# One dS unit in eight turned by TensorE instead of the crossbar, in the attention backward of an adaLN transformer block

## The chip, the cores and the metric

The kernel runs on one core of a Trainium2 chip. The metric is the device time of one execution in microseconds. The kernel before took 2854.23 us, the median of four runs (2842.84, 2850.54, 2857.91, 2863.89). The core has five engines that run side by side: TensorE (PE, matrix products, with its weight loads listed apart as PEld), VectorE (DVE), ScalarE (ACT), GpSimd (POOL) and SyncE (SP, which here issues most DMAs). SBUF is the working memory; PSUM holds the results of matmuls in eight banks of 2 KB per partition.

## The reference

A transformer block with adaptive layer norm (one sequence of 2048 tokens, width 512, 32 heads of 16) is run forward and backward; the outputs are the block's result and the gradients of nine inputs.

```python
scale = Dh ** (-0.5)                       # Dh = 16, H = 32
scores = einsum('bhqd,bhkd->bhqk', q, k) * scale
p = softmax(scores)
o = einsum('bhqk,bhkd->bhqd', p, v)
...
x = x + ga * (o @ wo)                      # o with the heads side by side
h = layernorm(x) * (1 + cb) + sb
x = x + gb * (relu(h @ w1 + b1) ** 2 @ w2 + b2)
_out, _vjp = jax.vjp(_f, A_x, A_wqkv, A_wo, B_w1, B_b1, B_w2, B_b2, c, w_mod)
return (_out, *_vjp(grad_out))
```

The part that matters here is the backward of the attention: with P the probabilities, it needs dV = P^T dO, dP = dO V^T, dS = P * (dP - rowsum(dO * O)), dQ = dS K and dK = dS^T Q, for each head a 2048 x 2048 matrix of scores.

## The kernel before

The forward, the MLP and its backward take the first 1256 us or so, the attention backward (`attn_bwd`) the next 1444, and `phase6`, the input and weight gradients, the rest.

`attn_bwd` loops over eight quads of heads (`g`), two pairs of heads in each (`jp`), four chunks of 512 keys (`c`) and 16 blocks of 128 queries (`ib`). One turn of the innermost loop is called a unit here: 8 x 2 x 4 x 16 = 1024 units, each with two heads (`a`). Four units with the same chunk (`G = 4`) form a group: 256 groups. Queries lie on the partitions, keys in the free dimension.

For a unit the program issues, in this order:
- for each of the two heads, the scores (L1265, a matmul of 64 rows into a `st` bank of PSUM) and the dP of the unit before (L1218, into half of a `dp` tile; the softmax correction is folded into extra rows of the operands). The `st` pool has two banks, so the exponentials free them one by one; `dp` has two tiles.
- on ScalarE the exponential of each head's scores (L1269, 128x512, PSUM to SBUF, into `pu`)
- on VectorE the product dS = dP * P of the unit before (L1223, 128x1024, into a quarter of the `ds` tile of its group). `ds` has three buffers.
- after every second unit, the dK and dV matmuls of two earlier units (`kv`, L1179, eight matmuls); after the units between, the dQ matmuls of two earlier units (`dq`, L1199, 16 matmuls).

dK and dV use dS as it lies. dQ needs it turned, with keys on the partitions. After the product of a group's fourth unit, which stands in the first unit of the next group, SP issues one DMA transpose of the whole group, through the crossbar on the way from SBUF to SBUF (L1227: 128 x 4096 elements into the 32 blocks of 128x128 of a `dsT` tile, four buffers). The dQ matmuls wait in a list (`pendq`) until more than eight units stand in it, and so a group's dQ is issued in the first and third unit of the third group after it. SP's queue holds, besides the 256 transposes, the loads of the next heads' operands, one between two groups.

After the last query block of a chunk VectorE scales and copies the dK/dV sums (L1182, `kvT`, 64 times); after the last chunk of a pair of heads `turn` transposes the whole of `kvT` on TensorE (L1188, 16 transposes into a `dp` tile) and ScalarE copies the result out twice (L1192), 16 times in all.

TensorE and SP keep the order written in the program. VectorE and ScalarE follow the order in which the program's tiles become ready to the framework, and each waits on semaphores of the engines it depends on.

Of the kernel before, what the change touches and what calls it, by code (L numbers as in the profile page):

```python
# [18 lines left out]
P = 128  # L19
# [68 lines left out]
class K:  # L88
# [1060 lines left out]
    def attn_bwd(self):  # L1149
# [9 lines left out]
        G = 4  # L1159
        W = 4 * DH  # L1160
        with ExitStack() as es:
            dtp = es.enter_context(tc.tile_pool(name="p5dt", bufs=4))
            kvp = es.enter_context(tc.tile_pool(name="p5kv", bufs=1))
            stp = es.enter_context(tc.tile_pool(name="p5st", bufs=2, space=PSUM))
            dpp = es.enter_context(tc.tile_pool(name="p5dp", bufs=2, space=PSUM))
            accp = es.enter_context(tc.tile_pool(name="p5acc", bufs=1, space=PSUM))
            acckv = accp.tile([P, 512], F32, name="acckv")
            nc.vector.memset(acckv[:], 0.0)
            accq = accp.tile([P, ST, 2, DH], F32, name="accq")
            masked, kvs = self.masked, self.kvs  # L1170
            pend, pendq = [], []

            def kv(u):
                (T, g, jp, c, ib, kvT, pu, ds) = u
                for j, (n, src) in enumerate((("Q", ds), ("dO", pu))):
                    for a in range(2):
                        r = 64 * j + 32 * a
                        col = (2 * jp + a) * DH
                        nc.tensor.matmul(acckv[r:r + DH, :], lhsT=T[n][:, ib, col:col + DH], rhs=src[:, a, :],  # L1179
                                         start=(ib == 0), stop=(ib == ST - 1))  # L1180
                if ib == ST - 1:
                    nc.vector.tensor_scalar(kvT[:, 512 * c:512 * (c + 1)], acckv[:], kvs[:], None, ALU.mult)  # L1182

            def turn(g, jp, kvT):
                h0 = 4 * g + 2 * jp
                tp = dpp.tile([P, ST, P], BF16, name="dp")
                for st in range(ST):
                    nc.tensor.transpose(tp[:, st, :], kvT[:, st * P:(st + 1) * P], self.ident[:])  # L1188
                v = tp[:].rearrange("p s (t a e) -> p t s a e", t=2, a=2)
                for t, dst in enumerate((self.dk_t, self.dv_t)):  # L1190
                    d = dst[:, :, h0 * DH:(h0 + 2) * DH].rearrange("p s (a d) -> p s a d", a=2)
                    nc.scalar.copy(d, v[:, t, :, :, 0:DH])  # L1192

            def dq(u, heads):
                (T, g, jp, c, ib, i, dsT) = u
                for a in heads:
                    col = (2 * jp + a) * DH
                    for sub in range(4):
                        nc.tensor.matmul(accq[:, ib, a, :], lhsT=dsT[:, (i * 2 + a) * 4 + sub, :],  # L1199
                                         rhs=T["K"][:, 4 * c + sub, col:col + DH],  # L1200
                                         start=(c == 0 and ib == 0 and a == 0 and sub == 0), stop=False,
                                         skip_group_check=True)
                if c == SC - 1 and ib == ST - 1 and 1 in heads:
                    h0 = 4 * g + 2 * jp
                    d = self.dq_t[:, :, h0 * DH:(h0 + 2) * DH].rearrange("p s (a d) -> p s a d", a=2)
                    nc.vector.tensor_scalar(d, accq[:], self.scale, None, ALU.mult)

            def kv_two():
                for u in pend[:2]:
                    kv(u)  # L1210
                (T, g, jp, c, ib, kvT, pu, ds) = pend[1]
                del pend[:2]
                return (g, jp, kvT) if c == SC - 1 and ib == ST - 1 else None

            def dP(dp, u, a):
                (T, g, jp, c, ib, kvT, pu, dsg, i) = u
                rd = slice(64 - 64 * jp, 128 - 64 * jp)
                nc.tensor.matmul(dp[:, a, :], lhsT=T["dOT"][rd, ib * P:(ib + 1) * P],  # L1218
                                 rhs=masked["VT"][2 * jp + a][rd, 512 * c:512 * (c + 1)], start=True, stop=True)

            def dS(dp, u):
                (T, g, jp, c, ib, kvT, pu, dsg, i) = u
                nc.vector.tensor_tensor(dsg[:, i], dp[:], pu[:], ALU.mult)  # L1223
                pend.append((T, g, jp, c, ib, kvT, pu, dsg[:, i]))
                if i == G - 1:
                    dsT = dtp.tile([P, 8 * G, P], BF16, name="dsT")
                    nc.sync.dma_start_transpose(dsT[:], dsg[:].rearrange("p i a k -> p (i a k)"))  # L1227
                    for i in range(G):
                        pendq.append((T, g, jp, c, ib - G + 1 + i, i, dsT))

            T = self.T0
            turnq, last = [], None
            for g in range(NQ):
                for jp in range(2):
                    pieces = []
                    if jp == 0:
                        pieces = self.pair_pieces(g, 1)
                    elif g + 1 == NQ:
                        for st in range(0, ST, 2):
                            pieces.append((self.xhat1_6[:, st:st + 2, :], self.xhat1_d.rearrange("(st p) d -> p st d", p=P)[:, st:st + 2, :]))  # L1240
                        for kt in range(self.DT):
                            pieces.append((self.wq_6[:, kt, :], self.io["A_wqkv"][kt * P:(kt + 1) * P, :]))
                    else:
                        Tn, pieces = self.load_group(g + 1)
                        pieces = self.pair_pieces(g + 1, 0) + pieces
                    kvT = kvp.tile([P, S], BF16, name="kvT")
                    for c in range(SC):
                        c0 = 512 * c
                        for ib0 in range(0, ST, G):
                            if pieces and (c or ib0):  # L1250
                                nc.sync.dma_start(*pieces.pop(0))
                            dsg = self.dsp.tile([P, G, 2, 512], BF16, name="ds")
                            for i in range(G):
                                ib = ib0 + i
                                q = slice(ib * P, (ib + 1) * P)
                                if turnq and i == 2:
                                    turn(*turnq.pop(0))
                                pu = self.pup.tile([P, 2, 512], BF16, name="pu")

                                if last:  # L1260
                                    dp = dpp.tile([P, 2, 512], F32, name="dp")
                                for a in range(2):
                                    stt = stp.tile([P, 512], F32, name="st")
                                    rs = slice(64 * jp, 64 * jp + 64)
                                    nc.tensor.matmul(stt[:], lhsT=T["QT"][rs, q], rhs=masked["KT"][2 * jp + a][rs, c0:c0 + 512],  # L1265
                                                     start=True, stop=True)
                                    if last:
                                        dP(dp, last, a)
                                    nc.scalar.activation(pu[:, a, :], stt[:], ACT.Exp, scale=self.scale)  # L1269
                                if last:  # L1270
                                    dS(dp, last)
                                last = (T, g, jp, c, ib, kvT, pu, dsg, i)
                                if i % 2 == 1 and len(pend) >= 4:
                                    r = kv_two()
                                    if r:
                                        turnq.append(r)
                                elif i % 2 == 0 and len(pendq) > 2 * G:
                                    for _ in range(4 if len(pendq) > 3 * G else 2):
                                        dq(pendq.pop(0), [0, 1])
                T = Tn  # L1280
            dp = dpp.tile([P, 2, 512], F32, name="dp")
            for a in range(2):
                dP(dp, last, a)
            dS(dp, last)
            while len(pend) > 2:
                kv_two()
            turn(*kv_two())
            while pendq:
                dq(pendq.pop(0), [0, 1])
# [254 lines left out]
```

The softmax here doesn't subtract the row's maximum and nothing guards it: scores larger than these inputs give would overflow.

## Time and profile before

| | |
|---|---|
| median of four runs | 2854.23 us |
| profiled execution | 2841.99 us (span 2840.2) |
| TensorE busy | 2518.3 us, 89% |
| ScalarE busy | 2214.8 us, 78% |
| VectorE busy | 1787.5 us, 63% |
| exponentials of the backward, L1269 | 1109.0 us, 2048 of 595 ns |
| dS products, L1223 | 1213.9 us, 1024 of 1220 ns |
| dsT transposes by DMA, L1227 | 256, median 8.0 us from issue to landing |
| mean granted TensorE clock | 0.966 |

Busy times of one engine add up only where its instructions do not overlap: an exponential of 595 ns starts some 0.54 us after the one before. "Idle before" is the time that an engine stood still just ahead of an instruction, and the name after the arrow is what ended it. A matmul's shown length (0.39 us for 512 columns) is longer than the distance between two of them, and two that use different halves of the array lie beside each other. SP's transposes show some 5.3 us each, which holds their wait for the products.

### The profile page before, as it was taken

Reading aid. Unit: us, or ns where it says so; the run is one execution under the profiler, and the core shown is the slowest. Engines: PE = TensorE matmul, PEld = TensorE weight load, DVE = VectorE, ACT = ScalarE, POOL = GpSimd, SP = SyncE. Lnnn points to the kernel's source line nnn. Section 1 sums busy time; section 2 is a strip of 40 time slices with the busy share of each in tenths; the row PEclk is TensorE's granted clock in tenths of the full one; section 3 lists DMA queues with packets and bytes.
Section 4 is the critical chain, followed back from the end, with each engine's and each line's share of the span. In section 5 each row is a group of like instructions: output and inputs, shape, how many; then the busy total and the mean of one; then the engine's idle time right before and its main releaser. Section 6 shows DMA issues by size and latency. Waiting matters only on the chain. (4 is left out here: it accounts for less than half of the span.)

```text
span 2840.2 us, 72244 instructions
## 1 busy us (share of the span) xinstructions
PE 2518.3 (89%) x29963; PEld 1212.8 (43%) x30186; DVE 1787.5 (63%) x2712; ACT 2214.8 (78%) x3376; POOL 361.3 (13%) x633
## 2 busy tenths in 40 slices
PE   5999799999999989979888888888888889899897
PEld 2555455555555545723333333333333333333343
DVE  4222323323312345649898888998988989889847
ACT  4999799999999975238787777887877878778623
POOL 2244201310321122420000000000000000000021
PEclk9999899999999999989999999999999999999999
DMA  4367743420631355989999999999999999999977
GB/s 150 89 148 161 156 89 90 119 67 20 152 86 40 101 157 162 204 198 200 210 200 206 206 201 210 198 204 209 198 208 202 200 209 195 209 204 205 213 193 194
DMA packets 1331346, 472.86 MB, mean 166 GB/s; under 512 B 1266471, under 2 KB 1293609, under 8 KB 1331017
## 3 DMA queue, kind: packets, MB, share of 16 engines
q1 hardware_dynamic: 1299816, 379.40, 72.6%
q0 software_dynamic: 29088, 86.21, 10.3%
q8 instruction: 236, 3.87, 0.5%
q10 hardware_dynamic: 2112, 2.62, 0.3%
q14 instruction: 94, 0.76, 0.1%
HBM read 83.30 MB, written 67.11 MB: 53 GB/s over the span
## 5 line engine op out<-in xcount | busy, mean ns | idle before, releaser
L1269 ACT ACTIVATE pu<-st 128x512 bf16<-128x512 f32 x2048 | 1109.0, 595 | 306.5 <-PE dp L1218 273.7
L1223 DVE TENSOR_TENSOR ds<-dp,pu 128x1024 bf16<-128x1024 f32 x1024 | 1213.9, 1220 | 187.4 <-PE dp L1218 152.1
L331 ACT ACTIVATE pu<-st 128x1024 bf16<-128x1024 f32 x1024 | 955.7, 1046 | 25.9 <-PE st L328 21.3
L328 PE MATMUL st<-QTm,KTq 128*128 128x512 bf16 x1940 | 586.3, 379 | 37.2 <-ACT pu L331 7.7
L293 PEld LDWEIGHTS <-pu 128*128 128x128 bf16 x8192 | 344.7, 96 | 249.5 <-issue 24.1
L1265 PE MATMUL st<-m,q 64*128 64x512 bf16 x1024 | 367.1, 399 | 20.8 <-ACT pu L1269 8.9
L1265 PE MATMUL st<-m,QTq 64*128 64x512 bf16 x1024 | 364.7, 395 | 15.6 <-ACT pu L1269 4.5
L1218 PE MATMUL dp<-m,q 64*128 64x512 bf16 x1024 | 370.2, 404 | 0.1
L1199 PEld LDWEIGHTS <-dsT 128*128 128x128 bf16 x8192 | 240.9, 96 | 302.7 <-DMA dsT<-ds 191.1
L293 PE MATMUL accbank<-Vaug,pu 128*128 128x17 bf16 x8192 | 349.0, 171 | 22.0 <-DVE O L301 15.0
L1218 PE MATMUL dp<-m,dOTq 64*128 64x512 bf16 x1024 | 366.1, 400 | 0.0
L328 PEld LDWEIGHTS <-KTq 128*128 128x128 bf16 x2048 | 194.7, 96 | 206.0 <-issue 140.8
L1199 PE MATMUL accq<-Kg,dsT 128*128 128x16 bf16 x4096 | 143.7, 171 | 75.8 <-DMA dsT<-ds 75.6
L1199 PE MATMUL accq<-q,dsT 128*128 128x16 bf16 x4096 | 144.3, 171 | 72.0 <-DMA dsT<-ds 71.7
L1434 POOL DMA_DIRECT2D wmod<-in_w_mod_dram x6 | 4.6, 772 | 1452.2 <-DVE kvT L1182 1446.0
L1179 PE MATMUL acckv<-pu,q 128*16 128x512 bf16 x1024 | 163.3, 401 | 0.0
L1179 PE MATMUL acckv<-ds,q 128*16 128x512 bf16 x1024 | 163.3, 401 | 0.0
L1179 PE MATMUL acckv<-ds,Qg 128*16 128x512 bf16 x1024 | 161.2, 396 | 0.7 <-DVE ds L1223 0.7
L1179 PE MATMUL acckv<-pu,dOg 128*16 128x512 bf16 x1024 | 161.2, 396 | 0.0
L1218 PEld LDWEIGHTS <-q 64*128 64x128 bf16 x1024 | 90.4, 94 | 113.5 <-issue 104.1
L1218 PEld LDWEIGHTS <-dOTq 64*128 64x128 bf16 x1024 | 89.5, 94 | 103.3 <-issue 94.9
L300 DVE RECIPROCAL rl<-accbank 128x4 f32<-128x4 f32 x128 | 22.9, 179 | 164.8 <-PE accbank L293 164.7
(309 smaller groups left out, 2336.0 us busy)
## 6 DMA issues: line engine op xcount, KB each, us to landing
KTq<-KTq_d POOLq DMA_DIRECT2D x24, 512.0 KB, 3.7
duT_d<-auT POOLq DMA_DIRECT2D x4, 1792.0 KB, 8.2
aT_d<-rT POOLq DMA_DIRECT2D x4, 1792.0 KB, 13.0
KTq_d<-KTq SPq DMA_DIRECT2D x32, 128.0 KB, 2.1
QTq_d<-ev_fm SPq DMA_DIRECT2D x32, 128.0 KB, 2.3
VTq_d<-vT POOLq DMA_DIRECT2D x4, 1024.0 KB, 6.2
O_d<-O POOLq DMA_DIRECT2D x4, 1024.0 KB, 5.6
m<-KTq_d SPq DMA_DIRECT2D x32, 128.0 KB, 3.5
```

What stands on the lines that cost most here:

```text
L293: nc.tensor.matmul(acc[:, a, sub, :], lhsT=pu[:, a, sub * P:(sub + 1) * P], rhs=Vaug[:, kb, h, :], start=(kb == 0 and a == 0 and sub == 0) ...
L300: nc.vector.reciprocal(self.rl[:, st0:st0 + 4, h], acc[:, a, :, DH])
L328: nc.tensor.matmul(stt[:, a, :], lhsT=KT[:, kb * P:(kb + 1) * P], rhs=QTm[2 * jp + a][:], start=True, stop=True)
L331: nc.scalar.activation(pu[:], stt[:], ACT.Exp, scale=self.scale)
L1179: nc.tensor.matmul(acckv[r:r + DH, :], lhsT=T[n][:, ib, col:col + DH], rhs=src[:, a, :], start=(ib == 0), stop=(ib == ST - 1))
L1199: nc.tensor.matmul(accq[:, ib, a, :], lhsT=dsT[:, (i * 2 + a) * 4 + sub, :], rhs=T["K"][:, 4 * c + sub, col:col + DH], start=(c == 0 and i ...
L1218: nc.tensor.matmul(dp[:, a, :], lhsT=T["dOT"][rd, ib * P:(ib + 1) * P], rhs=masked["VT"][2 * jp + a][rd, 512 * c:512 * (c + 1)], start=Tru ...
L1223: nc.vector.tensor_tensor(dsg[:, i], dp[:], pu[:], ALU.mult)
L1265: nc.tensor.matmul(stt[:], lhsT=T["QT"][rs, q], rhs=masked["KT"][2 * jp + a][rs, c0:c0 + 512], start=True, stop=True)
L1269: nc.scalar.activation(pu[:, a, :], stt[:], ACT.Exp, scale=self.scale)
L1434: nc.gpsimd.dma_start(wmod[:], wmod_v[:, :, j * D:(j + 1) * D])
```

## The change

The groups are taken in turn; every second one (`ib0 // G` odd, so query blocks 4 to 7 and 12 to 15) has its first unit turned by TensorE, 128 units of 1024. At the end of such a group's fourth unit, after the dK and dV matmuls, a new function `turn_ds` allocates the group's `dsT` tile, issues eight transposes of 128x128 (two heads, four blocks of keys) into a tile of the `st` pool (one bank, 128 x 1024 in bf16), and copies four blocks out by ScalarE and four by VectorE. The DMA transpose of that group, issued as before after its fourth product, then moves the other three units: 24 blocks in place of 32. `dq` reads the tile as before.

```diff
             def dS(dp, u):
-                (T, g, jp, c, ib, kvT, pu, dsg, i) = u
+                (T, g, jp, c, ib, kvT, pu, dsg, i, grp) = u
                 nc.vector.tensor_tensor(dsg[:, i], dp[:], pu[:], ALU.mult)
                 pend.append((T, g, jp, c, ib, kvT, pu, dsg[:, i]))
                 if i == G - 1:
-                    dsT = dtp.tile([P, 8 * G, P], BF16, name="dsT")
-                    nc.sync.dma_start_transpose(dsT[:], dsg[:].rearrange("p i a k -> p (i a k)"))
+                    i0 = len(grp)
+                    dsT = grp[0] if i0 else dtp.tile([P, 8 * G, P], BF16, name="dsT")
+                    nc.sync.dma_start_transpose(dsT[:, 8 * i0:, :], dsg[:, i0:].rearrange("p i a k -> p (i a k)"))
                     for i in range(G):
                         pendq.append((T, g, jp, c, ib - G + 1 + i, i, dsT))
+
+            def turn_ds(dsg, grp):
+
+                dsT = dtp.tile([P, 8 * G, P], BF16, name="dsT")
+                tp = stp.tile([P, 8, P], BF16, name="st")
+                for b in range(8):
+                    nc.tensor.transpose(tp[:, b, :], dsg[:, 0, b // 4, b % 4 * P:(b % 4 + 1) * P], self.ident[:])
+                nc.scalar.copy(dsT[:, 0:4, :], tp[:, 0:4, :])
+                nc.vector.tensor_copy(dsT[:, 4:8, :], tp[:, 4:8, :])
+                grp.append(dsT)
...
-                            dsg = self.dsp.tile([P, G, 2, 512], BF16, name="ds")
+                            dsg, grp = self.dsp.tile([P, G, 2, 512], BF16, name="ds"), []
...
                                 elif i % 2 == 0 and len(pendq) > 2 * G:
                                     for _ in range(4 if len(pendq) > 3 * G else 2):
                                         dq(pendq.pop(0), [0, 1])
+                                if i == G - 1 and ib0 // G % 2:
+                                    turn_ds(dsg, grp)
```

More of the change, by code (lines that the diff above doesn't have):

```diff
@@ L1221, in dS @@
             def dS(dp, u):
-                (T, g, jp, c, ib, kvT, pu, dsg, i) = u
+                (T, g, jp, c, ib, kvT, pu, dsg, i, grp) = u
                 nc.vector.tensor_tensor(dsg[:, i], dp[:], pu[:], ALU.mult)
@@ L1271, in attn_bwd @@
                                     dS(dp, last)
-                                last = (T, g, jp, c, ib, kvT, pu, dsg, i)
+                                last = (T, g, jp, c, ib, kvT, pu, dsg, i, grp)
                                 if i % 2 == 1 and len(pend) >= 4:
```

## The prediction

> **Bound.** I read the page first, then the busy time of the stage that the change touches, then its waits, then its order in time.
>
> ```profile
> span 2840.2 us, 72244 instructions
> ...
> DVE  4222323323312345649898888998988989889847
> ...
> DMA  4367743420631355989999999999999999999977
> ```
>
> From slice 18 on (about 1256 us) the attention backward runs: VectorE is at 8 to 9 tenths and the DMA engines at 9 until 2700 us.
>
> ```profile
> 1256.00:2700.00 1444.00, 1264.30 (x16566) 517.23 (x16565) 1258.57 (x1107) 1121.66 (x2075) 0.79 (x1) 0.95 1.14 204
> ```
>
> The columns are length, then busy PE, weight loads, VectorE, ScalarE, GpSimd, then the granted clock (0.95) and the DMA share. There are 1024 units, 256 groups of four, 128 pairs of groups; the change acts once a pair. A pair takes 1444/128 = 11.28 us, of which VectorE works 9.83, TensorE 9.88, ScalarE 8.76. Three engines are near full and none is full. What fills the rest are waits:
>
> ```profile
> PEld L1199 <- DMA dsT<-ds: 186.5, 140, 3.8
> ...
> DVE ds L1223 <- PE dp L1218: 152.1, 186, 3.4
> ...
> ACT dk_t L1192 <- PE dp L1188: 16.5, 16, 3.5
> DVE ds L1223 <- ACT pu L1269: 14.8, 19, 3.1
> ```
>
> TensorE stands 140 times at the dQ matmuls until a turned dS lands (186.5 us); the products on VectorE then come late. VectorE's own idle time before the product is 152.1 + 14.8 + 3.0 (a third releaser in the same answer) = 170 us. That is the cost of the crossbar as the end sees it, less what is not the crossbar's: the turning of dK and dV, 16 times, below.
>
> Where no wait falls, this is the order in time (start, length):
>
> ```profile
> 2003.20 0.37 PE L1265 MATMUL st<-m,q 64*128 64x512 bf16 x1
> ...
> 2003.36 2.21 ACT L1269 ACTIVATE pu<-st 128x512 bf16<-128x512 f32 x4 [0.21 <-PE dp L1218]
> 2003.52 0.11 PEld L1179 LDWEIGHTS <-q 128*16 128x16 bf16 x8 [0.23 <-issue]
> ...
> 2004.06 0.39 PE L1265 MATMUL st<-m,q 64*128 64x512 bf16 x1
> ...
> 2004.50 0.37 PE L1265 MATMUL st<-m,q 64*128 64x512 bf16 x1
> ...
> 2004.51 0.39 PE L1218 MATMUL dp<-m,q 64*128 64x512 bf16 x1
> ```
>
> Four exponentials fill 2.21 us of a period of two units of 2.4 us; the second score block (2004.50) starts 0.04 us after an exponential frees its bank; the product on VectorE starts 0.50 us after the last dP matmul (2005.01; also 2001.29 after 2000.79), and VectorE's products follow each other every 1.2 us (12 in 14.47 us). So TensorE, ScalarE and VectorE are all within a few per cent of that pace: a delay put into this loop is not made up later.
>
> **Removed.** One unit in eight leaves the crossbar: 128 x 0.25 MB of 256 MB; SP still issues 256 transposes in the same order among the same loads, every other one a quarter shorter. Its ceiling is the stall: 170 us less the dK/dV turns. Those are priced by the trace itself:
>
> ```profile
> 1617.45 1.07 PE L1188 MATMUL dp<-ident,kvT 128*128 128x128 bf16 x16
> ...
> 1618.56 0.58 ACT L1192 COPY dk_t<-dp 128x512 bf16<-128x512 bf16 x1 [0.67 <-PE dp L1188]
> ...
> 1619.04 0.59 ACT L1192 COPY dv_t<-dp 128x512 bf16<-128x512 bf16 x1
> 1619.20 1.23 DVE L1223 TENSOR_TENSOR ds<-dp,pu 128x1024 bf16<-128x1024 f32 x1 [0.86 <-PE dp L1218]
> ...
> 1619.52 2.17 ACT L1269 ACTIVATE pu<-st 128x512 bf16<-128x512 f32 x4
> ...
> 1621.19 1.23 DVE L1223 TENSOR_TENSOR ds<-dp,pu 128x1024 bf16<-128x1024 f32 x1 [0.77 <-ACT pu L1269]
> ```
>
> Sixteen transposes hold TensorE from 1617.45 to the next scores at 1618.45, two copies hold ScalarE until 1619.52, and VectorE idles 0.86 + 0.77 = 1.63 us for it: 16 x 1.63 = 26 us. So at most 170 - 26 = 144 us, 1.13 a pair, can be won; floor of the gain is 0. Is the stall really gone? A transpose's landing is needed two groups after its last product: at 2014.69 a dQ got one 8.6 us after that product's end, at 2021.71 another after 10.8. The room without stalls is 7 products x 1.2 = 8.4 us, plus 0.7 in the half that hold a kvT copy; with one turn inside it gets 1.25 longer (next part), 9.7 to 10.4, and the transposes are lighter. So most waits go, the latest landings may keep some: I take 20 us kept, 124 won. Nor does DMA throughput come next: seven eighths of 11.28 is 9.9 us a pair.
>
> **Added.** Per pair: 8 transposes on TensorE, 16 in 1.00 us above, so 0.50 us (64 us in all); one copy each on ScalarE and VectorE, for which the trace has the same shape from PSUM:
>
> ```profile
> L577 DVE COPY fT<-tp x4: 405/424/425, 1045.8 to 1063.4; 128x512 bf16<-128x512 bf16 x4
> L577 ACT COPY fT<-tp x4: 566/585/585, 1046.1 to 1060.4; 128x512 bf16<-128x512 bf16 x4
> ```
>
> 0.424 us on VectorE (54 us in all) and 0.585 on ScalarE (75). The sums do not decide, the order does. The transposes stand after the dK/dV matmuls of a group's fourth unit, ahead of the next unit's scores, and write one of the two score banks. In the built program the VectorE copy waits for the ScalarE copy (same bank), and because the first bank is still held, the next unit's two score blocks both get the second bank: its second score matmul waits for the exponential of its first. Taking 2003.20 above as the fourth unit: TensorE is free at 4.06 (2004.06); transposes to 4.56, the last issued at 4.50; ScalarE's copy starts 0.17 later (1618.39 to 1618.56 in the turn above), 4.67; the next exponential 0.48 later (1619.04 to 1619.52), 5.15; it lasts 0.55, 5.70; the second score block 0.04 later, 5.74, its dP 5.75, the product 0.50 later, 6.25. In the trace that product is at 5.01. The turn costs 1.25 us. VectorE's copy (about 5.35 to 5.77) lies in the hole this makes and costs nothing; were the hole shorter than 0.42 it would cost up to 54 us. The next unit follows at VectorE's 1.2 us pitch with ScalarE and TensorE just in time, so the 1.25 stay.
>
> Bounds: without the shared bank ScalarE would go straight on (exponentials at 5.15 and 5.70, the unit after that 0.6 late): 0.6 us. The dK/dV turn, with twice the transposes and copies, cost 1.63. I take 1.25, as the waits of the built program force it.
>
> Two rules against the rows. The trace has 1.00 us for 16 transposes; the Trainium skill ("VectorE: DVE Perf Modes", The three transpose paths) gives 390 ns for one on TensorE, by which eight would take 3.1 us, as an estimate 128 x 2.6 = 335 us more than by the row. I go by the row: back to back they overlap. And the skill's "PSUM — Partial Sum Buffer" (PSUM bank collisions raise a hardware error) says that ScalarE and VectorE must not read one bank at the same time; no row of this trace shows two engines at one bank, and the waits of the built program agree with the rule. By it splitting the copy saves nothing: 0.585 and 0.424 follow each other.
>
> **Sum.** 128 x 1.25 = 160 us added, 124 won: +36. The profiled execution was 2842 us (span 2840.2), so 2878; the median of the four runs lies 12 above it, at 2854, and I predict for that: 2890.
>
> **Rivals.**
> - *The turn is nearly hidden.* At 0.6 us a turn costs 77 us; against it 124 to 144 won: -47 to -67, some 2797 (faster). For it: ScalarE is only 78% busy. Against: its exponentials sit on the loop, as the 0.04 us shows. It decides below 0.97 us a turn (124/128).
> - *The stall takes up the turn.* The landings stay where they are (the time in flight being set by latency) and the loop over them keeps its 11.28 a pair, the turn lying inside the wait: within 14 us of 2854. For it: TensorE's waits are 1.46 us a pair, about a turn. Against: VectorE's waits fall in 186 + 19 places of various size, so not every turn meets one.
> - *The turn costs as much as a dK/dV turn and stalls stay in part.* 1.63 x 128 = 209, less 90 to 124: +85 to +119, 2939 to 2973. For it: the same engines in the same order. Against: half the work.
> - *The change does not do what it says*: excluded as far as the order goes, the built program has 128 sets of eight transposes and two copies.
>
> **Chances.** A change of 0.5%, 14 us, is about what measuring this kernel tells from none. Forecast (turn 1.1 to 1.5, stall mostly gone: 2865 to 2925) 0.58, of which 0.50 is slower by more than 14 us and 0.08 not. Hidden turn 0.24, faster. Stall takes up the turn 0.06, same. Dear turn 0.12, slower. So faster 0.24, same 0.14, slower 0.62. The 80% range leaves out the lower half of the hidden-turn case and the far part of the dear one: 2815 to 2945.
>
> **Signs.** Right: TensorE's wait for dsT under 60 us; ScalarE idle before its new copy about 0.2 us; VectorE idle before the product after a turn about 1.2 us less its copy; a fresh wait of the second score block for an exponential (0.5 us and more, 128 times); a pair at 11.4 to 11.6 us. Wrong: waits for dsT still above 120 us; the product after a turn less than 0.9 us late; transposes at more than 0.1 us each.

## The result and the profile after

The changed kernel takes 2846.7 us (median; 2840.6 to 2857.0), the kernel before 2853.6 in the runs made beside it: ratio 0.9975, 95% interval 0.9967 to 0.9984. That is a quarter of a per cent faster, 7 us, within what the prediction called no change. 2890 was forecast, slower.

The first view is the page of the changed kernel (span, and the busy tenths of 40 slices), then the busy time of the backward: length, PE, weight loads, VectorE, ScalarE, GpSimd, granted clock, DMA share, GB/s.

```profile
span 2847.2 us, 74441 instructions
...
DVE  4222423323312345649988898888988899888957
...
DMA  4367733520531356989999999999999999999977
```

```profile
1260.00:2710.00 1450.00, 1314.75 (x17612) 583.12 (x17610) 1304.25 (x1235) 1201.14 (x2205) 0.79 (x1) 1.00 0.99 180
```

The backward is as long as before, about 1447 us from the first product to the end of the last (1442 before), but it is filled otherwise: VectorE 1304 us of work where it had 1259, ScalarE 1201 where it had 1122. The DMA share is 0.99 instead of 1.14, with 180 GB/s instead of 204, and TensorE's clock is 1.00 instead of 0.95. (The profiled execution of before was one of its quickest, 2842 us against the median of 2854; this matters below.)

The waits of the backward after the change (engine, line, what it waited for, us in all, times, longest):

```profile
PE st L1276 <- ACT pu L1280: 117.3, 146, 3.5
...
DVE ds L1223 <- PE dp L1218: 87.2, 146, 3.3
...
ACT dsT L1238 <- PE st L1237: 50.0, 128, 0.5
DVE dsT L1239 <- ACT dsT L1238: 30.2, 81, 0.4
...
PEld L1199 <- DMA dsT<-ds: 4.8, 9, 1.7
```

TensorE's wait for turned dS has gone from 186.5 us to 4.8. In its place stands the wait that the prediction built from the program: the second score block after a turn waits for the exponential of the first. Of the 117.3 us in 146 places, 105 lie at the 128 turns (0.82 us each in the mean). One turn in the order of time shows the whole chain (start, length):

```profile
2002.93 0.37 PE L1276 MATMUL st<-m,q 64*128 64x512 bf16 x1
...
2003.79 0.62 PE L1237 MATMUL st<-ident,ds 128*128 128x128 bf16 x8
...
2004.34 0.39 PE L1276 MATMUL st<-m,q 64*128 64x512 bf16 x1
...
2004.45 0.58 ACT L1238 COPY dsT<-st 128x512 bf16<-128x512 bf16 x1 [0.48 <-PE st L1237]
2004.93 0.60 ACT L1280 ACTIVATE pu<-st 128x512 bf16<-128x512 f32 x1
2005.07 0.42 DVE L1239 COPY dsT<-st 128x512 bf16<-128x512 bf16 x1 [0.29 <-ACT dsT L1238]
2005.59 0.37 PE L1276 MATMUL st<-m,q 64*128 64x512 bf16 x1 [0.85 <-ACT pu L1280]
...
2006.03 1.22 DVE L1223 TENSOR_TENSOR ds<-dp,pu 128x1024 bf16<-128x1024 f32 x1 [0.54 <-PE dp L1218]
```

From the last score block of the fourth unit (2002.93) it is 0.86 us to the transposes, 1.52 to ScalarE's copy, 2.00 to the exponential, 2.66 to the second score block and 3.10 to the product. The prediction's hand-made chain, from the same point, had 0.86, 1.47, 1.95, 2.54 and 3.05. So the turn was foreseen well. What it was set against was not.

### The profile page after: what moved, and what is told of

Its sections match the earlier page's. It is cut to its first block, busy times and chain, and to the rows that moved or that the text cites. A ratio compares the mean times of both kernels' runs of the same rounds, so it can differ in the third digit from the quotient of the medians.

```text
span 2847.2 us, 74441 instructions
## 1 busy us (share of the span) xinstructions
PE 2569.5 (90%) x30987; PEld 1280.3 (45%) x31210; DVE 1832.1 (64%) x2840; ACT 2293.9 (81%) x3504; POOL 361.4 (13%) x633
## 5 line engine op out<-in xcount | busy, mean ns | idle before, releaser
L1280 ACT ACTIVATE pu<-st 128x512 bf16<-128x512 f32 x2048 | 1126.1, 596 | 180.2 <-PE dp L1218 117.2
L293 PE MATMUL accbank<-Vaug,pu 128*128 128x17 bf16 x8192 | 349.2, 171 | 18.8 <-DVE O L301 11.6
L1218 PE MATMUL dp<-m,q 64*128 64x512 bf16 x1024 | 364.2, 386 | 0.0
L1179 PE MATMUL acckv<-ds,Qg 128*16 128x512 bf16 x1024 | 154.0, 381 | 0.6 <-DVE ds L1223 0.6
L1179 PE MATMUL acckv<-pu,q 128*16 128x512 bf16 x1024 | 154.5, 382 | 0.0
L1179 PE MATMUL acckv<-ds,q 128*16 128x512 bf16 x1024 | 154.5, 382 | 0.0
L1179 PE MATMUL acckv<-pu,dOg 128*16 128x512 bf16 x1024 | 154.0, 381 | 0.0
```

Source lines behind the costliest of these rows:

```text
L293: nc.tensor.matmul(acc[:, a, sub, :], lhsT=pu[:, a, sub * P:(sub + 1) * P], rhs=Vaug[:, kb, h, :], start=(kb == 0 and a == 0 and sub == 0) ...
```

## The experiments

Each ran beside the kernel before on the same chip; ratios are to that, with 95% intervals.

### The relief alone, the turn alone

The first is the kernel before with the crossbar relieved by an eighth, and nothing turned in exchange:

```diff
-nc.sync.dma_start_transpose(dsT[:], dsg[:].rearrange("p i a k -> p (i a k)"))
+i0 = ib // G % 2
+nc.sync.dma_start_transpose(dsT[:, 8 * i0:, :], dsg[:, i0:].rearrange("p i a k -> p (i a k)"))
...
-    pendq.append((T, g, jp, c, ib - G + 1 + i, i, dsT))
+    pendq.append((T, g, jp, c, ib - G + 1 + i, max(i, i0), dsT))
```

> The kernel before with the crossbar relieved and no turn by TensorE: in every second group only three units are transposed, and the dQ matmuls of the group's first unit read the second unit's blocks in its place (dQ is therefore wrong for one unit in eight; the number of matmuls is the same). Theory A (the stall is worth about 150 us and goes as soon as the crossbar has an eighth less to move): 145 to 160 us faster than before, about 2700, TensorE's wait for dsT under 20 us. Theory B (the lighter transposes alone are not enough, the room that the turn adds to the loop is needed too): 40 to 110 us faster, with 50 us or more of wait left.

Measured: 2732.6 us, 0.9582 [0.9553, 0.9611], 119 us faster. It lies between the two theories; 50 us or more of wait, as the second has it, are left. In 1320 us of its backward the weight loads of dQ still waited this much for the crossbar:

```profile
PEld L1199 <- DMA dsT<-ds: 77.6, 78, 2.8
```

The second has the turns, and a crossbar that moves all four units of every group, over the turned blocks too:

```diff
-i0 = len(grp)
-dsT = grp[0] if i0 else dtp.tile([P, 8 * G, P], BF16, name="dsT")
-nc.sync.dma_start_transpose(dsT[:, 8 * i0:, :], dsg[:, i0:].rearrange("p i a k -> p (i a k)"))
+dsT = grp[0] if grp else dtp.tile([P, 8 * G, P], BF16, name="dsT")
+nc.sync.dma_start_transpose(dsT[:], dsg[:].rearrange("p i a k -> p (i a k)"))
```

> The changed kernel with its turns (transposes, both copies) and the crossbar not relieved: the DMA transpose of every group moves all four units, over the turned blocks too. Theory A (the relief takes the stall away, the turn adds 1.25 us each): the turns cost 160 us, of which the longer loop hides some of the stall: 2900 to 3010, with more than 60 us of wait for dsT left. Theory B (the turn itself makes the room, the relief is hardly needed): within 25 us of the changed kernel, 2830 to 2870, with under 40 us of wait left.

Measured: 2886.3 us, 1.0129 [1.009, 1.0169], 35 us slower than before, again between the two. So 128 turns put in front of an unrelieved crossbar cost only 35 us: most of a turn fell into time that was being waited away (idle time of the dQ weight loads and matmuls for dsT: 85 us, where the kernel before had 338). And the changed kernel is 114 us slower than the relief alone, not 160. The parts do not add up because turn and stall cover each other; each has to be priced with the other gone.

### No wait at the dQ matmuls, and no crossbar at all

In the next kernel the dQ matmuls read the identity and wait for nothing; the 256 transposes run as before.

```diff
-lhsT=dsT[:, (i * 2 + a) * 4 + sub, :]
+lhsT=self.ident[:]
```

> The kernel before with the dQ matmuls reading the identity in place of dsT, so that they wait for no transpose (dQ is wrong); the 256 DMA transposes run as before. This is the whole worth of the stall. Theory A: 145 to 165 us faster than before, 2690 to 2710, granted clock in the stage near 1.0. If the products' buffers, which are also held until a transpose has read them, stall VectorE in its place: less than 100 us faster, with VectorE waiting for the transposes.

Measured: 2844.9 us, 0.9971 [0.9955, 0.9986]: hardly anything, although the wait that the prediction had quoted is gone altogether. The second expectation held, that another place takes it over. Its waits, in 1320 us of the backward:

```profile
PE dp L1218 <- DVE ds L1223: 98.1, 108, 2.9
DVE ds L1223 <- DMA dsT<-ds: 72.2, 47, 3.3
```

Now VectorE waits for the transposes, to get a `ds` buffer back, and TensorE for VectorE. The traffic in 900 us of the backward (1600 to 2500 us), of the kernel before and then of this one:

```profile
DMA packets 664810, 183.09 MB, mean 203 GB/s; under 512 B 658940, under 2 KB 658940, under 8 KB 664700
```

```profile
DMA packets 664334, 182.96 MB, mean 203 GB/s; under 512 B 658464, under 2 KB 658464, under 8 KB 664224
```

The same 203 GB/s. The wait at dQ was only where the pace of the transposes came to the surface.

Leaving out the DMA transposes as well gives the backward without the crossbar; doing the same in the changed kernel gives the bare price of the turns.

```diff
-dsT = dtp.tile([P, 8 * G, P], BF16, name="dsT")
-nc.sync.dma_start_transpose(dsT[:], dsg[:].rearrange("p i a k -> p (i a k)"))
+dsT = None
```

> The kernel before without any DMA transpose of dS; the dQ matmuls read the identity (dQ is wrong), their number is the same. This gives the backward with no stall of any kind from the crossbar. Theory A (the whole stall is worth 155 to 170 us, of which the relief by an eighth alone won 119): 2680 to 2700. Theory C (the relief alone had already won everything there is, and the turn costs only the 114 us between that run and the changed kernel): 2725 to 2740.

> The changed kernel without any DMA transpose of dS; the turns and their copies stay, the dQ matmuls read the identity (dQ is wrong). Against the run with no crossbar and no turn this is the bare price of the 128 turns. Theory A (1.25 us each): 150 to 165 us more than that run, 2840 to 2855, no different from the changed kernel by more than 10 us, because that one has no stall left. Theory C (about 0.9 us each): 100 to 125 us more.

Measured: without the crossbar 2669.3 us, 0.9357 [0.9342, 0.9373], 185 us faster than before, more than either theory allowed. With the turns 2837.9 us, 0.9945 [0.9928, 0.9962]: 168.6 us more, 1.32 us a turn, a little above the upper end of the first expectation. The changed kernel (2846.7) is 9 us above that. The balance of the change in medians is therefore 169 (turns) - 185 (stall) + 9 (left over) = -7.

Where the 185 were is read from the rows of the product's group over the whole kernel (busy, mean ns, idle before it): before, without the crossbar, and in the kernel without a wait at dQ.

```profile
L1223 DVE TENSOR_TENSOR ds<-dp,pu 128x1024 bf16<-128x1024 f32 x1024 | 1213.9, 1220 | 187.4 <-PE dp L1218 152.1 <-ACT pu L1269 14.8 <-PE st L1265 3.0
```

```profile
L1223 DVE TENSOR_TENSOR ds<-dp,pu 128x1024 bf16<-128x1024 f32 x1024 | 1193.1, 1218 | 42.7 <-PE dp L1218 16.1 <-ACT pu L1268 13.9 <-PE accq L1199 0.5
```

```profile
L1223 DVE TENSOR_TENSOR ds<-dp,pu 128x1024 bf16<-128x1024 f32 x1024 | 1196.6, 1219 | 205.2 <-DMA dsT<-ds 84.4 <-PE dp L1218 54.7 <-ACT pu L1269 36.7
```

Without the crossbar the idle time is 144.7 us less. The busy time is 20.8 us less as well, although one product is as long as before. Most of this is overlap: a product that follows at once starts some 0.08 us before the one ahead of it ends, and a product that comes late does not. 1024 times the mean length is 1249 us before and 1247 without the crossbar, so the overlap is 35 us before and 54 without. The lower clock of TensorE is not what lengthened the busy time: the third kernel has 0.95 too, and 1196.6. Another 8 us lie behind the last product (from its end to the end of the span, 143.2 us before, 135.4 here), where before the last transposes are waited for.

A stretch of VectorE in the kernel without the crossbar shows that the loop itself is no faster there:

```profile
1918.38 18.87 DVE L1223 TENSOR_TENSOR ds<-dp,pu 128x1024 bf16<-128x1024 f32 x16
```

These are 16 products behind a copy of the dK/dV sums. The first ones catch up, 1.14 us from start to start up to 1926.34; from there to 1936.03 the pace is 1.21 us, as in the prediction's stretch of the kernel before (12 in 14.47 us).

### The kernel before, profiled again

> The kernel before, profiled once more: the first profiled execution (2842 us) lay under every one of the runs but a few. Expected 2850 to 2860, about 150 to 200 us of wait for dsT, granted clock 0.95 in the backward. If its clock and its waits are as in the changed kernel, the first profile was no fair sample.

The second profiled execution took 2863.2 us with a span of 2861.5, and in 1320 us of its backward TensorE waited 167.3 us for dsT. The first one, 2842.0, lay 12 us under the median: a stall read from it is about that much too small. The clock was 0.95 in both.

### Is it the crossbar's rate, or the time in flight?

If it were the time in flight of one large transpose against the buffers, smaller transposes with the same buffer space would help. Groups of two units, twice as many buffers:

```diff
-self.dsp = self.open_pool("p5ds", bufs=3)
+self.dsp = self.open_pool("p5ds", bufs=6)
...
-G = 4
+G = 2
...
-dtp = es.enter_context(tc.tile_pool(name="p5dt", bufs=4))
+dtp = es.enter_context(tc.tile_pool(name="p5dt", bufs=8))
...
-if pieces and (c or ib0):
+if pieces and (c or ib0) and ib0 % 4 == 0:
...
-if turnq and i == 2:
+if turnq and ib % 4 == 2:
...
-elif i % 2 == 0 and len(pendq) > 2 * G:
-    for _ in range(4 if len(pendq) > 3 * G else 2):
+elif i % 2 == 0 and len(pendq) > 8:
+    for _ in range(4 if len(pendq) > 12 else 2):
```

> The kernel before, no turn by TensorE, with the crossbar's transposes cut from four units to two (512 of half the size; twice as many ds and dsT buffers of half the size, dQ still issued eight to ten units behind, the loads of operands and the dK/dV turn at the same places). Theory L (the stall is the time in flight of one 1 MB transpose against the room of three ds and four dsT buffers, not the crossbar's rate): a transpose of half the size lands sooner and its room grows by two units: 80 to 150 us faster than before, 2700 to 2775. Theory R (the crossbar is at its rate: 5.6 us per 1 MB): no change, 2845 to 2865, or slower for twice the issues.

Measured: 2897.8 us, 1.0152 [1.0128, 1.0176], slower. A transpose landed after 4.8 us instead of 8.2 (medians in 1600 to 2500 us), and nothing was gained; the traffic in the same window was

```profile
DMA packets 648064, 176.22 MB, mean 196 GB/s; under 512 B 642962, under 2 KB 642962, under 8 KB 647954
```

So the kernel before ran at the rate of its transposes: 5.6 us for each MB, 1442 us for 256 MB. The DMA share is 1.14 in this kernel, in the kernel before and without the dQ wait, and smaller transposes made the rate a little worse.

Whose rate this is, is less clear than the word crossbar says. SP's queue is full too:

```profile
1997.45 47.44 SPq L1227 DMA_TRANSPOSE dsT<-ds  x9
```

This is the kernel before: nine transposes issued one behind the other, 5.27 us each. This time holds no wait for the product, since every transpose starts on SP after the end of its group's last product, and 238 of the 256 start more than 0.1 us after it. The 256 issues take 1341 us in all, 1348 without the dQ wait, and the 512 of half the size 1343. In 900 us (1600 to 2500) SP was busy issuing for 878 in the kernel before, 752 in the changed one. Whether the issue on SP sets the pace or is itself held up by the crossbar and the DMA engines, no run separates; "the crossbar's rate" below means the two together.

### The turn made cheaper

Three versions of the changed kernel test what a turn costs, and one its number. In the first, VectorE copies everything out:

```diff
-nc.scalar.copy(dsT[:, 0:4, :], tp[:, 0:4, :])
-nc.vector.tensor_copy(dsT[:, 4:8, :], tp[:, 4:8, :])
+nc.vector.tensor_copy(dsT[:, 0:8, :], tp[:])
```

> The changed kernel with the whole turned unit copied out by VectorE in one instruction and none by ScalarE. VectorE has a hole of about 1 us at a turn, its copy of 128x1024 should take some 0.85 us; ScalarE then goes straight on to the next exponential, but the two score blocks after the turn still share a bank. If the chain through ScalarE is what a turn costs: about 1.05 us a turn in place of 1.3, 20 to 35 us faster than the changed kernel, 2810 to 2825. If VectorE's copy delays the product: 0 to 40 us slower.

Measured: 2829.1 us, 0.9906 [0.9886, 0.9925], 18 us less than the changed kernel; the direction was right, the size a little under what was expected. One turn of it:

```profile
2003.69 0.60 ACT L1279 ACTIVATE pu<-st 128x512 bf16<-128x512 f32 x1 [0.64 <-PE dp L1218]
2003.78 0.68 DVE L1238 COPY dsT<-st 128x1024 bf16<-128x1024 bf16 x1
2004.34 0.37 PE L1275 MATMUL st<-m,q 64*128 64x512 bf16 x1 [0.68 <-ACT pu L1279]
...
2004.86 9.55 DVE L1223 TENSOR_TENSOR ds<-dp,pu 128x1024 bf16<-128x1024 f32 x8 [0.39 <-PE dp L1218]
```

The second score block still waits for an exponential: the shared score bank is what is left. In the second version the turned unit goes into a `dp` tile, one half to each of its two banks, and no score bank is held:

```diff
-tp = stp.tile([P, 8, P], BF16, name="st")
+tp = dpp.tile([P, ST, P], BF16, name="dp")
-nc.tensor.transpose(tp[:, b, :], dsg[:, 0, b // 4, b % 4 * P:(b % 4 + 1) * P], self.ident[:])
+nc.tensor.transpose(tp[:, b + b // 4 * 4, :], dsg[:, 0, b // 4, b % 4 * P:(b % 4 + 1) * P], self.ident[:])
-nc.vector.tensor_copy(dsT[:, 4:8, :], tp[:, 4:8, :])
+nc.vector.tensor_copy(dsT[:, 4:8, :], tp[:, 8:12, :])
```

> The changed kernel with the turned unit in a dp tile (two banks, one for each half) in place of a score bank: the score banks are not held, the two copies need not follow each other. If the shared score bank is what makes a turn cost 1.25 us, a turn falls to about 0.6 (the ScalarE copy still stands before the next exponentials): 60 to 85 us faster than the changed kernel, 2760 to 2790, part of the gain given back to stalls that come back. If not, it is within 15 us of the changed kernel, or slower because dP waits for the bank.

Measured: 2791.2 us, 0.9789 [0.9767, 0.9811], faster than both kernels: 63 us under before, 55 under the changed one. One turn of it:

```profile
2000.38 0.59 ACT L1238 COPY dsT<-dp 128x512 bf16<-128x512 bf16 x1 [0.38 <-PE dp L1237]
2000.87 1.09 ACT L1280 ACTIVATE pu<-st 128x512 bf16<-128x512 f32 x2
2000.87 0.37 PE L1218 MATMUL dp<-m,q 64*128 64x512 bf16 x1 [0.21 <-DVE ds L1223]
...
2001.00 0.42 DVE L1239 COPY dsT<-dp 128x512 bf16<-128x512 bf16 x1 [0.18 <-ACT dsT L1238]
...
2001.50 1.23 DVE L1223 TENSOR_TENSOR ds<-dp,pu 128x1024 bf16<-128x1024 f32 x1
```

The two exponentials now follow each other at once. The product before it started at 1999.61 and this one at 2001.50, 1.89 us apart (1.90 is the median of the 128 turns) instead of 1.2: 0.7 us a turn, close to the lower bound of 0.6 that the prediction had worked out for a turn without the shared bank. 128 such turns are 90 of the 122 us by which this version lies above the one without a crossbar; some stall is back, with 47 us of idle time for dsT. VectorE's copy still waits for ScalarE's, though the halves lie in two banks. So this wait does not need a shared bank, to which the prediction had put it down; why the built program has it, these runs do not show.

The last two have a turn in every fourth group (64 turns), in the form of the change and in the form with the `dp` tile:

```diff
-if i == G - 1 and ib0 // G % 2:
+if i == G - 1 and ib0 // G == 2:
```

> The changed kernel with a turn in every fourth group in place of every second (64 turns, one unit in sixteen off the crossbar). Theory A (turns at 1.25 us, stalls that a sixteenth less of crossbar work and half the turns mostly remove): 80 us of turns saved, 20 to 50 of stall back: 2790 to 2830. If the stall comes back as fast as turns go: 2840 to 2855.

> The version with the turned unit in a dp tile, with a turn in every fourth group in place of every second (64 turns, one unit in sixteen off the crossbar). Reading so far: the crossbar runs at its rate (a backward of 1442 us for 256 MB), compute alone takes 1277 us and a turn in a dp tile about 0.7 more. Crossbar 15/16 of 1442 = 1352, compute 1277 + 45 = 1322: the crossbar bounds again, 90 us faster than before at best, less some 20 to 40 for the two getting in each other's way: 2785 to 2805, that is about as the version with 128 turns (2791). Clearly below 2785: the two overlap better than that. Above 2805: the crossbar's pace, not the turns, decides here.

Measured: 2806.2 us, 0.9840 [0.9817, 0.9863], and 2792.4 us, 0.9784 [0.9759, 0.9809]. With dear turns half as many are 40 us better; with cheap ones there is no difference between 64 and 128. Both forms with 64 turns are again near the crossbar's rate: both moved 198 GB/s (203 before, 180 in the changed kernel, 187 in the form with the `dp` tile and 128 turns). In the second of them the idle time ended by dsT (weight loads and matmuls of dQ together) is 155 us, against 47 with 128 turns and 338 in the kernel before. An estimate from 5.6 us per MB, a backward of 1277 us without the crossbar and 0.7 us a turn: with 64 turns the crossbar needs 1352 us and compute 1322, with 128 the crossbar 1262 and compute 1367. So the longer of the two changes sides in between, and the sums are nearly the same.

## Why the prediction was wrong

The forecast was +36 us, -7 was measured. The side was wrong. The value lies inside the range by luck: the turn was taken 9 us too low, the ceiling of the stall 41 too low and the stall kept 11 too high, and two of the three push the forecast up: 41 + 11 - 9 is the 43 between +36 and -7. Its sum was 160 (turns) - 144 (ceiling of the stall) + 20 (stall kept). The runs price the same three at 169, 185 and 9.

- **The turn (160, measured 169)** held, in its mechanism and nearly in its size: the shared bank, the ScalarE copy ahead of the exponential, VectorE's copy inside the hole, no making up afterwards. 1.25 us was worked out, 1.32 measured in the kernels without crossbar. The rival of a nearly hidden turn is excluded for this form; at 0.7 us it came true for the form in a `dp` tile.
- **The ceiling of the stall (144, measured 185)** is the step that failed, in the words "at most 170 - 26 = 144 us, 1.13 a pair, can be won". The idle time ahead of the products was read well: 144.7 us of it went when the crossbar did. But idle time was not the whole price. A product that comes late also loses its overlap with the one before, and 20.8 us went from the time that the profile counts as busy; 8 us lay behind the last product, and 12 us were the difference between one quick profiled execution and the median, which the prediction added to the time but not to the stall. 144.7 + 20.8 + 7.8 + 11.6 is 185. The free pace taken from the trace, 1.2 us a product, was right: it is 1.21 without the crossbar.
- **The stall kept (20, measured 9)** rested on the landing time against the room of two groups. That argument falls: it was the crossbar's rate that bound, as the run without a dQ wait and the one with smaller transposes show. With seven eighths of the work the crossbar needs, as an estimate, some 1262 us (7/8 of 1442), compute without a turn 1277. In the relief alone, then, the two nearly tie, and yet 63 us of stall stay (2732.6 - 2669.3); why a tie costs that much was not tested. (At the poorer rate of the half-size transposes, 1497 us for 256 MB, seven eighths would be 1310.) Compute with turns is 169 longer, and the crossbar falls out of the way. The prediction said that seven eighths of the rate was no bound, which was right, but did not use the rate to price the stall: 1442 - 1277 is 165 of the 185.
- **The rival in which the stall takes up the turn** gave the measured time (within 14 us of before) by another road: it kept the landings as the bound. In the changed kernel compute with turns is the bound, since it lies only 9 us above its version without any crossbar; that its time comes so near to before's is a coincidence of 169 and 185.
- **The signs** set down beforehand: the wait for dsT under 60 us (4.8), the fresh wait of the second score block (0.85 us in the turn shown, 117.3 in all), transposes far below 0.1 us each (eight in 0.55, 2003.79 to 2004.34) came true. So did VectorE's idle time around its copy, 0.29 + 0.54 = 0.83 us in the turn shown, where 1.2 less its copy was set down. ScalarE idled 0.48 us before its copy in the turn shown, not 0.2. A pair takes 1447/128 = 11.30 us, not 11.4 to 11.6.
- **The two rules weighed.** The row was right for the transposes, eight in 0.55 us and not 3.1. On the copies, the wait stands with two banks too, so these runs do not show that the bank is its reason.

For the crossbar itself the Trainium skill ("DMA: Bandwidth & Descriptors", Latency and other measured facts) has 261 GB/s for a DMA transpose with a non-contiguous middle dimension and 350 to 400 for a contiguous one. Here the engines moved 203 GB/s in the kernel before, and the same without the dQ wait, of which the transposes are 186 (256 MB of 2^20 bytes in 1442 us); the measurement decides.

## What to carry to other kernels

A stall is worth what the stage takes as it is less what it takes with the cause removed, not the idle time that names it: find the rate of the suspected resource (bytes per second, the same in every variant) and the pace of the stage without it, and take the larger of the two. When two resources nearly tie, the parts of a change do not add: the relief alone won 119 us and the turn alone lost 35, and together they gave 7. A helper that borrows a buffer of a double-buffered loop costs its engine time and the loop's overlap too; give it a buffer that stands free at that moment (here 55 us).

## What the runs showed of the hardware

- With the DMA transposes from SBUF to SBUF the engines moved 203, 203 and 196 GB/s (their loads included) in three kernels with different waits and sizes; 512 KB transposes were slower per byte than 1 MB ones (196 against 203). A transpose held SP for at least 4.8 us at 1 MB (before), 3.6 at 0.75 (changed kernel) and 1.6 at 0.5 (groups of two).
- TensorE's granted clock went with its waits: in the backward 0.94 to 0.95 in the kernels at the crossbar's rate (before, groups of two, no dQ wait), 0.99 with the relief alone, 1.00 with no crossbar and in the changed kernel. The Trainium skill ("TensorE: Matmul & The Clock Gate", Part 1: The HAM clock gate (the "warmup" mystery)) says that TensorE falls to half its clock after an idle window of about 3.4 us. The trace agrees on the half (its clock records hold 0.50 and 1.00; the longest score matmul before took 632 ns against a median of 377) but not on the condition: in the backward of the second profile of the kernel before, half the clock was granted 39 times, mostly for 3.4 us, while no idle stretch of TensorE there was longer than 3.1 us. The measurement decides.
- VectorE copied 128x1024 bf16 from PSUM in 681 ns and 128x512 in 424: the second half cost 257 ns. ScalarE took 1012 and 585 for the same two sizes.
